# Softmax weights of the first batch four pipeline slots sooner, and q of pairs 2 to 5 (and 7) transposed by the DMA crossbar instead of TensorE

## The chip, the cores and the metric

One core of a Trainium2 chip runs the whole kernel. The metric is the device time of one execution in microseconds. Most executions of one kernel agree within 0.3%. A ratio is the mean time of one kernel's fast runs over that of the other's of the same rounds, so it is not quite the ratio of the medians quoted beside it. "By crossbar" means that a DMA transfer does the transpose (`dma_start_transpose`), so that neither TensorE nor VectorE works for it.

## The reference, cut to what matters

```python
# attention: batch 8, heads 8, seq 576, head_dim 64
scores = scale * q @ k.T
thresh = max(scores) - tau
attn   = softmax(where(scores >= thresh, scores, -1e9))
o      = attn @ v                                # [8, 8, 576, 64]
# layers on x = o as [4608, 512]
h   = x @ w_in                                   # [512, 2048]
out = (h - tanh(h)) @ w_out                      # [2048, 512]
```

## The kernel before

The unit of work is a **pair**, two heads of one batch; there are 32, four per batch. A pair has nine score tiles, and one tile goes through each stage of a software pipeline per **slot**. In slot s the kernel makes scores of tile s+8, applies the threshold to tile s+5 (`kink`, ScalarE), makes the softmax weights of tile s (`weights`: transposes on TensorE or by crossbar, then an exponential on ScalarE) and attends with tile s-2. From slot 40 on, the layers of the finished batch are woven in.

Each pair needs preparation some slots ahead of its first tile: q and k are loaded, split into a high and a low half on GpSimd, and turned (transposed). Meanwhile the layer weights arrive in 16 pieces, which GpSimd casts to bf16.

```python
def split(p, t):                  # GpSimd, 2.6 us for each of q and k
    nc.gpsimd.tensor_scalar(...)                  # scale
    nc.gpsimd.tensor_copy(out=hl[:, :, 0, :], ...)      # high half
    nc.gpsimd.tensor_tensor(out=hl[:, :, 1, :], ...)    # low half

def q_by_dma(p):
    return p >= 2 * HPAIR and p % 2 == 1          # HPAIR = 4

def turn(p, t):
    if t == "q" and q_by_dma(p):
        nc.sync.dma_start_transpose(...)          # SP queue
        return
    ...                                           # nine TensorE transposes
    nc.vector.tensor_copy(out=m, in_=ps)          # one VectorE copy
    ...

# one piece of layer weights every fourth slot: cast the last one, load the next
wt_pool = pool("wt", 2)
if s + AHEAD in w_when:
    if loaded:
        w_cast()                                  # GpSimd
    piece = next(pieces, None)
    if piece:
        w_load(piece)                             # SP queue
```

After the first pair, every load of q, k, v and layer weights, every crossbar transpose and every store (but for two of the last ones) is issued by one queue, SP. Where q goes by crossbar its `turn` stands five slots ahead of the pair's first scores, otherwise three.

Of the kernel before, what the change touches and what calls it, by code (L numbers as in the profile page):

```python
# [18 lines left out]
def kernel(  # L19
# [26 lines left out]
    HPAIR = H // 2  # L46
    NPAIR = B * HPAIR
    DM_C = d_model // P
    DF_C = d_ff // P
    TPP = 9  # L50
    NTILE = NPAIR * TPP
# [3 lines left out]
    def on_pe(i):  # L55
        p, j = divmod(i, TPP)
        return p < HPAIR or p < 2 * HPAIR and j in (0, 1, 4, 5, 6)
# [3 lines left out]
    AHEAD = 8  # L61
    LDK = 16
    MASK = 5
    LAG = 2
# [165 lines left out]

    def q_by_dma(p):

        return p >= 2 * HPAIR and p % 2 == 1

    def turn(p, t):
        hl = hls.pop((p, t))
# [48 lines left out]
    def kind(j):  # L285

        return "M" if j == 4 else "A" if j in (0, 2, 5, 7) else "B"
# [41 lines left out]
    def shift(i):  # L329

        kd = kind(i % TPP)
        if kd == "A":
            return
        n = 2 if kd == "B" else 1
        mx = mxs.pop(i)
        nb = st_pool.tile([P, 2], F32, name="nb", tag="nb")
        nc.vector.tensor_scalar(  # L337
            out=nb[:, 0:n], in0=mx[:, 0:n], scalar1=-1.0, scalar2=tau,
            op0=ALU.mult, op1=ALU.add,
        )  # L340
        nbs[i] = nb[:, n - 1 : n]
        if kd == "B":
            nbs[i - 1] = nb[:, 0:1]
# [23 lines left out]
    def weights(i):  # L367


        kd = kind(i % TPP)  # L370
        n, off = {"A": (4, 0), "M": (5, 0), "B": (5, 4)}[kd]
        if on_pe(i):
            z = zts.pop(i)
            pl, tag = (ps_h, "h") if i % 2 and i < HPAIR * TPP else (ps_y, "y")
            ps = pl.tile([P, 5 * P], BF16, name="psZ", tag=tag)
            for c in range(n):
                nc.tensor.matmul(  # L377
                    out=ps[:, c * P : (c + 1) * P],
                    lhsT=z[:, (off + c) * P : (off + c + 1) * P],
                    rhs=ident_bf, is_transpose=True, start=True, stop=True,  # L380
                )
            if kd == "B":
                pt = pts.pop(i - 1)
            else:
                pt = p_pool.tile([P, TPP * P], FP16, name="pT")
            nc.scalar.activation(  # L386
                out=pt[:, off * P : (off + n) * P], in_=ps[:, 0 : n * P], func=ACT.Exp
            )
        elif kd == "A":
            return  # L390
        else:
            n += off
            pt = p_pool.tile([P, TPP * P], FP16, name="pT")
            nc.scalar.activation(  # L394
                out=pt[:, 0 : n * P], in_=zts.pop(i)[:, 0:n, :], func=ACT.Exp
            )
        pts[i] = pt

    def attend(i):

        p, j = divmod(i, TPP)
        kd, vb = kind(j), vbs[p % NV]
        if kd == "A":
            return
        if j in (1, 6):
            ops[p, int(j > 4)] = ps_o.tile([P, 6, D + 1], F32, name="psO", tag="o")
        po = ops[p, int(j > 4)]
        if kd == "M":
            pt = pts.pop(i)

            for c in range(5):
                nc.tensor.matmul(  # L412
                    out=po[:, 4:6, :], lhsT=pt[:, c * P : (c + 1) * P],
                    rhs=vb[:, :, c, :], start=(c == 0), stop=(c == 4),
                )
            return
        pt, hh = pts.pop(i), int(j > 4)

        for ab in range(2):
            blocks = [(4 * ab + ab + c, c) for c in range(4)]  # L420
            blocks.append((4, 4 + ab))
            for n, (blk, c) in enumerate(blocks):
                nc.tensor.matmul(  # L423
                    out=po[:, (j - 1 - 5 * hh) + ab, :],
                    lhsT=pt[:, blk * P : (blk + 1) * P], rhs=vb[:, hh, c, :],
                    start=(n == 0), stop=(n == 4),
                )
# [3 lines left out]
    def norm(p, hh):  # L431
        po = ops.pop((p, hh))
        if hh == 0:
            osb[p] = o_pool.tile([P, 5, 2, D], BF16, name="osb")
        n = 5 - hh
        rc = st_pool.tile([P, 5], F32, name="rc", tag="rc")
        nc.vector.reciprocal(out=rc[:, 0:n], in_=po[:, 0:n, D])
        nc.vector.tensor_tensor(  # L438
            out=osb[p][:, 0:4, hh, :], in0=po[:, 0:4, 0:D],
            in1=rc[:, 0:4].unsqueeze(2).to_broadcast([P, 4, D]), op=ALU.mult,  # L440
        )
        if hh == 0:
            nc.vector.scalar_tensor_tensor(
                out=osb[p][:, 4, :, :], in0=po[:, 4:6, 0:D], scalar=rc[:, 4:5],
                in1=own, op0=ALU.mult, op1=ALU.mult,
            )
# [3 lines left out]
    def emit_x(p):  # L450
        o = osb.pop(p)
        pf = ps_h.tile([P, 320], F32, name="psX", tag="h")
        ps = pf[:, 0:256].bitcast(BF16)
        for t in range(4):
            nc.tensor.matmul(
                out=ps[:, t * P : (t + 1) * P],
                lhsT=o[:, t, :, :].rearrange("p a d -> p (a d)"),
                rhs=ident_bf, is_transpose=True, start=True, stop=True,
            )

        nc.tensor.matmul(
            out=pf[:, 256:320], lhsT=o[:, 4, :, :].rearrange("p a d -> p (a d)"),
            rhs=fold, start=True, stop=True,
        )
        b = p // HPAIR
        if p % HPAIR == 0:
            xs[b] = x_pool.tile([P, DM_C, MB], BF16, name="xT")
        nc.vector.tensor_copy(out=xs[b][:, p % HPAIR, :], in_=ps[:, 0:512])
        nc.vector.tensor_copy(out=xR[:, p % HPAIR, b, :], in_=pf[:, 256:320])
# [17 lines left out]
    def bend():  # L487
        while halves:
            m, n, ps = halves.pop(0)
            th = t_pool.tile([P, MB], F32, name="th")  # L490
            nc.scalar.activation(out=th, in_=ps, func=ACT.Tanh)  # L491
            ths.append((m, n, ps, th))

    def shrink():
        while ths:
            m, n, ps, th = ths.pop(0)
            nc.vector.scalar_tensor_tensor(  # L497
                out=gs[m][:, n, :], in0=th, scalar=-1.0, in1=ps,
                op0=ALU.mult, op1=ALU.add,
            )  # L500
# [102 lines left out]
    def w_cast():  # L603
        flat, wt, i, cols = loaded.pop(0)
        nc.gpsimd.tensor_copy(out=flat[:, i * cols : (i + 1) * cols], in_=wt)
# [51 lines left out]
        if at < -AHEAD:  # L657
            plan.setdefault(-AHEAD, []).extend(plan.pop(at))

    kinks = {}  # L660
    for i in range(NTILE):
        kinks.setdefault(i // 2 * 2 + 2 - AHEAD if i < 4 else i - MASK, []).append(i)
    for s in range(-AHEAD, NTILE + LAG + 3):
        p, j = divmod(max(s, 0), TPP)
        if 0 <= s < NTILE and j == 2 + LAG and p % HPAIR == 0 and p >= HPAIR:
            assert not todo
            todo = layers(stage, False)
            share = len(todo) / (HPAIR * TPP - 2 - LAG)
            done, stage = 0.0, stage + 1
        if 0 <= s + AHEAD - 1 < NTILE:  # L670
            shift(s + AHEAD - 1)
        if 0 <= s + AHEAD < NTILE:
            scores(s + AHEAD)
        if s == 1 - AHEAD:
            for t in ("k", "q", "ks"):
                turn_first(t, 1)
        for i in kinks.pop(s, []):
            kink(i)
        bend()
        if 0 <= s < NTILE:  # L680
            weights(s)
            if todo:
                done += share
                if j == TPP - 1 and p % HPAIR == HPAIR - 1:
                    done = 1e9
                while todo and done >= 1:
                    todo.pop(0)()
                    done -= 1
        if s == 0:
            nc.vector.tensor_tensor(  # L690
                out=fold, in0=ident_bf[:, 0:64], in1=ident_bf[:, 64:P], op=ALU.add
            )
        shrink()
        for store in stores[:-1]:
            store()
        del stores[:-1]
        if 0 <= s - LAG < NTILE:
            attend(s - LAG)
            pp, jj = divmod(s - LAG, TPP)
            if jj == 4:  # L700
                norm(pp, 0)
            if jj == 8:
                norm(pp, 1)
        pp, jj = divmod(s - LAG, TPP)
        if jj == 1 and 0 < pp <= NPAIR:
            emit_x(pp - 1)
        for step in plan.pop(s, []):
            step()
        if True:
            if s + AHEAD in w_when:  # L710
                if loaded:
                    w_cast()
                piece = next(pieces, None)
                if piece:
                    w_load(piece)
# [47 lines left out]
```

## Time and profile before

| | before |
|---|---|
| median, lowest, highest of 3 runs | 545.71, 544.46, 546.08 us |
| span of the profiled run | 542.9 us |
| TensorE, VectorE, ScalarE, GpSimd busy | 93%, 82%, 81%, 54% |
| first batch (no layers yet) | about 7 to 72 us |
| GpSimd in 19 to 40 us | 19.88 of 21 us |

### The profile page before, as it was taken

To read this page: it belongs to the slowest core of one execution; us is meant where nothing else is said; L and a number is where in the kernel's file an instruction comes from. 1 tells how busy PE (TensorE), PEld (TensorE's weight loads), DVE (VectorE), ACT (ScalarE), POOL (GpSimd) and SP (SyncE) were. 2 spreads that over 40 slices of the span, in tenths; PEclk is the share of its full clock that TensorE was granted. 3 is DMA by queue.
4 is the path that set the end of the run, shared out by engine and by line. 5 is a ranking of instruction groups with operands and counts; after the bars stand their busy time and mean duration, and the time that the engine had idled before them with its cause. 6 is when DMAs were issued, how large, how long until landed. Compare 5 with 4: busy or idle time off the path is not lost.

```text
span 542.9 us, 12962 instructions
## 1 busy us (share of the span) xinstructions
PE 507.5 (93%) x4722; PEld 290.3 (53%) x4790; DVE 447.1 (82%) x1196; ACT 439.3 (81%) x630; POOL 290.7 (54%) x390
## 2 busy tenths in 40 slices
PE   5888888889999899999999999999999999899997
PEld 3566655555555555555555555555555555444444
DVE  4999999898888899889988989989989988544440
ACT  4899999998898888889888989899888989633330
POOL 7899987765456666557555755666655730000000
PEclk9999999998999999999999999999999999999999
DMA  7554688679697988789988999999999965310103
GB/s 211 168 182 145 205 202 175 148 131 197 141 173 160 175 169 199 163 191 195 181 188 172 177 200 186 165 171 191 192 177 179 200 127 117 83 41 39 40 39 77
DMA packets 202239, 85.13 MB, mean 157 GB/s; under 512 B 169792, under 2 KB 194624, under 8 KB 202176
## 3 DMA queue, kind: packets, MB, share of 16 engines
q1 hardware_dynamic: 201584, 83.89, 72.7%
q8 instruction: 37, 0.61, 0.5%
q10 hardware_dynamic: 592, 0.43, 0.3%
q14 instruction: 26, 0.21, 0.1%
HBM read 36.70 MB, written 9.44 MB: 85 GB/s over the span
## 4 chain that ended last, share of the span: by engine, by line
PE 67%; DVE 19%; POOL 6%; ACT 4%; issue 3%; DMA 0%; ACTq 0%; SPq 0%; DVEq 0%; POOLq 0%
PE psY L504 19%; PE psH L478 17%; PE psS L313 14%; DVE sc L323 9%; PE psO L423 5%; DVE g L497 3%; PE psS L303 3%; PE ps_k L227 3%; PE psHt L478 3%; DVE nb L337 2%; ACT z L357 2%; DVE osb L438 1%; POOL kS L256 1%; PE ps_q L227 1%; PE psO L412 1%
## 5 line engine op out<-in xcount | busy, mean ns | idle before, releaser
L323 DVE TENSOR_SCALAR_CACHE_REDUCE sc<-psS 128x576 f32<-128x576 f32 x288 | 215.3, 749 | 16.4 <-PE psS L313 11.0
L357 ACT ACTIVATE z<-sc,nb 128x576 bf16<-128x576 f32 x256 | 194.2, 771 | 21.9 <-DVE nb L337 21.3
L256 POOL COPY kS<-kT 64x1152 f16<-64x1152 f16 x62 | 70.9, 1143 | 135.8 <-DVE nb L337 133.2
L504 PE MATMUL psY<-w_out_sb,g 128*128 128x512 bf16 (+1 forms) x556 | 138.4, 373 | 2.2 <-issue 0.8
L394 ACT ACTIVATE pT<-zT 128x1152 f16<-128x1152 bf16 (+1 forms) x128 | 137.3, 1073 | 0.0
L478 PE MATMUL psH<-xT,w_in_sb 128*128 128x512 bf16 x451 | 118.0, 379 | 6.5 <-DVE g L497 4.4
L313 PE MATMUL psS<-kT,qT 128*128 128x512 f16 (+1 forms) x512 | 105.6, 288 | 11.2 <-DVE sc L323 9.2
L491 ACT ACTIVATE th<-psH 128x512 f32<-128x512 f32 x128 | 75.5, 590 | 39.2 <-PE psH L478 37.0
L313 PEld LDWEIGHTS <-qT 128*128 128x128 f16 x1024 | 73.1, 98 | 61.3 <-issue 14.5
L497 DVE SCALAR_TENSOR_TENSOR g<-th,psH 128x512 bf16<-128x512 f32 x128 | 87.2, 681 | 18.4 <-ACT th L491 18.4
L313 PE MATMUL psS<-kS,qT 128*128 128x512 f16 x496 | 101.9, 287 | 0.1
L478 PEld LDWEIGHTS <-w_in_sb 128*128 128x128 bf16 x576 | 49.4, 98 | 60.7 <-issue 7.2
L504 PEld LDWEIGHTS <-g 128*128 128x128 bf16 x592 | 51.0, 98 | 56.6 <-issue 2.9
L423 PEld LDWEIGHTS <-pT 128*128 128x128 f16 x1280 | 55.7, 98 | 25.0 <-issue 1.4
L423 PE MATMUL psO<-vb,pT 128*128 128x65 bf16 x1280 | 61.5, 194 | 0.9 <-ACT pT L394 0.6
L337 DVE TENSOR_SCALAR nb<-mx 128x2 f32<-128x2 f32 (+1 forms) x160 | 49.1, 307 | 2.5
L386 ACT ACTIVATE pT<-psZ 128x640 f16<-128x640 bf16 (+1 forms) x56 | 37.6, 671 | 5.1 <-PE psZ L377 5.0
L180 POOL TENSOR_TENSOR qhl<-qraw,qhl 128x576 f16<-128x576 f32 x31 | 39.7, 1281 | 2.6
L180 POOL TENSOR_TENSOR khl<-kraw,khl 128x576 f16<-128x576 f32 x31 | 39.7, 1281 | 2.6
L250 DVE COPY kT<-ps_k 128x1152 f16<-128x1152 f16 x31 | 23.4, 756 | 13.6 <-PE ps_k L227 13.2
L514 DVE COPY yo<-psY 128x512 f32<-128x512 f32 (+1 forms) x31 | 21.1, 679 | 11.3 <-PE psY L504 6.4
L438 DVE TENSOR_TENSOR osb<-psO,rc 128x256 bf16<-128x256 f32 x64 | 27.2, 424 | 2.2
(77 smaller groups left out, 508.4 us busy)
## 6 DMA issues: line engine op xcount, KB each, us to landing
vraw<-in_v_dram SPq DMA_DIRECT2D x32, 256.0 KB, 3.4
out_dram<-yo SPq DMA_DIRECT2D x32, 256.0 KB, 3.0
kraw<-in_k_dram SPq DMA_DIRECT2D x31, 256.0 KB, 3.2
qraw<-in_q_dram SPq DMA_DIRECT2D x31, 256.0 KB, 3.6
wt<-in_moe_w_in_dram SPq DMA_DIRECT2D x8, 512.0 KB, 4.7
wt<-in_moe_w_out_dram SPq DMA_DIRECT2D x8, 512.0 KB, 4.1
zT<-z SPq DMA_TRANSPOSE x104, 3.5
kraw<-in_k_dram SPq DMA_DIRECT2D x32, 32.0 KB, 2.8
```

The lines of the kernel that those rows point to most:

```text
L180: nc.gpsimd.tensor_tensor(out=hl[:, :, 1, :], in0=x, in1=hl[:, :, 0, :], op=ALU.subtract)
L256: nc.gpsimd.tensor_copy(out=o, in_=i)
L313: nc.tensor.matmul(out=ps[:, dst], lhsT=lhs, rhs=kk[:, src], start=(n == 0), stop=(n == 1),)
L323: nc.vector.tensor_scalar(out=sc, in0=ps[:, lo : lo + S], scalar1=SC, scalar2=None, op0=ALU.mult, op1=ALU.max, accum_out=mx[:, c : c + 1],)
L337: nc.vector.tensor_scalar(out=nb[:, 0:n], in0=mx[:, 0:n], scalar1=-1.0, scalar2=tau, op0=ALU.mult, op1=ALU.add,)
L357: nc.scalar.activation(out=z, in_=sc, func=ACT.Prelu, bias=nb, scale=1.0, alpha=STEEP)
L394: nc.scalar.activation(out=pt[:, 0 : n * P], in_=zts.pop(i)[:, 0:n, :], func=ACT.Exp)
L423: nc.tensor.matmul(out=po[:, (j - 1 - 5 * hh) + ab, :], lhsT=pt[:, blk * P : (blk + 1) * P], rhs=vb[:, hh, c, :], start=(n == 0), stop=(n ...
L478: nc.tensor.matmul(out=ps, lhsT=w_in_sb[:, c, n * P : (n + 1) * P], rhs=xs[m][:, c, :] if m < B else xR[:, c, :, :], start=(c == 0), stop= ...
L491: nc.scalar.activation(out=th, in_=ps, func=ACT.Tanh)
L497: nc.vector.scalar_tensor_tensor(out=gs[m][:, n, :], in0=th, scalar=-1.0, in1=ps, op0=ALU.mult, op1=ALU.add,)
L504: nc.tensor.matmul(out=ps, lhsT=gs[m][:, n, ms * P : (ms + 1) * P], rhs=w_out_sb[:, n, cols], start=(n == 0), stop=(n == DF_C - 1),)
```

## The change

Two things. Weights, attention and normalization of the first batch (36 tiles) move four slots sooner, to fill the pipeline's ramp, and so does the output of its pairs 0 to 2; that of pair 3 stays at slot 39. And q of pairs 2 to 5 goes by crossbar; by the wording of the condition pair 7 does too.

```diff
     def q_by_dma(p):
-        return p >= 2 * HPAIR and p % 2 == 1
+        return p in (2, 3, 4, 5) or p > 5 and p % 2 == 1
...
+    for i in range(NTILE + 3):
+        at = i - 4 if i < HPAIR * TPP else i
+        atts.setdefault(at + LAG, []).append(i)
+        if i < NTILE:
+            wts.setdefault(at, []).append(i)
...
+        for i in wts.pop(s, []):
+            weights(i)
         if 0 <= s < NTILE:
-            weights(s)
...
-        if 0 <= s - LAG < NTILE:
-            attend(s - LAG)
-        ...                     # norm and emit_x of tile s - LAG
+        for i in atts.pop(s, []):
+            ...                 # attend, norm and emit_x of tile i
```

More of the change, by code (lines that the diff above doesn't have):

```diff
@@ L658 @@
             plan.setdefault(-AHEAD, []).extend(plan.pop(at))
-    kinks = {}
-    for i in range(NTILE):
-        kinks.setdefault(i // 2 * 2 + 2 - AHEAD if i < 4 else i - MASK, []).append(i)
+    kinks, wts, atts = {}, {}, {}
+    for i in range(NTILE + 3):
[3 more added lines that the diff above has]
+            wts.setdefault(at, []).append(i)
+            kinks.setdefault(i // 2 * 2 + 2 - AHEAD if i < 4 else i - MASK, []).append(i)
     for s in range(-AHEAD, NTILE + LAG + 3):
@@ L696 @@
         del stores[:-1]
-        if 0 <= s - LAG < NTILE:
-            attend(s - LAG)
-            pp, jj = divmod(s - LAG, TPP)
-            if jj == 4:
-                norm(pp, 0)
-            if jj == 8:
-                norm(pp, 1)
-        pp, jj = divmod(s - LAG, TPP)
-        if jj == 1 and 0 < pp <= NPAIR:
-            emit_x(pp - 1)
+        for i in atts.pop(s, []):
+            pp, jj = divmod(i, TPP)
+            if i < NTILE:
+                attend(i)
+            if i < NTILE and jj in (4, 8):
+                norm(pp, int(jj > 4))
+            if jj == 1 and pp:
+                emit_x(pp - 1)
         for step in plan.pop(s, []):
```

## The prediction

> **What bounds the kernel now.** I read the busy shares by stretch first, then the chain of waits, then the time lines of GpSimd, of the DMA-issuing queue (SP) and of TensorE. A pair is two heads of one batch: nine score tiles, nine slots of the software pipeline. Pairs 0 to 3 are the first batch, before the layers start. Busy time by stretch (columns: PE, weight load, DVE, ACT, POOL, then clock, DMA share, GB/s), cut at the first scores of pairs 3, 4, 5 and 6:
>
> ```profile
> 41.70:53.40 11.70, 10.28 (x149) 7.64 (x149) 11.13 (x32) 10.69 (x19) 11.11 (x14) 1.00 0.55 167
> 53.40:65.20 11.80, 10.36 (x153) 7.72 (x151) 11.49 (x33) 11.57 (x20) 11.21 (x15) 1.00 0.67 191
> 65.20:79.30 14.10, 12.01 (x142) 8.04 (x144) 13.64 (x35) 12.95 (x21) 12.56 (x17) 1.00 0.85 190
> ```
>
> VectorE, ScalarE and GpSimd are all at 91 to 98% here: no engine can lose a microsecond unnoticed. In the stretch 128 to 187 us TensorE has 57.67 of 59 us, so from the third batch on TensorE sets the pace, and what the change wins or loses by about 94 us is carried to the end unaltered.
>
> The chain of waits between 37 and 73 us runs through GpSimd almost without a break. GpSimd's own time line (start, length):
>
> ```profile
> 37.33 1.28 POOL L180 TENSOR_TENSOR qhl<-qraw,qhl 128x576 f16<-128x576 f32 x1
> 38.67 2.33 POOL L256 COPY kS<-kT 64x1152 f16<-64x1152 f16 x2
> ...
> 42.33 2.03 POOL L605 CAST w_in_sb<-wt 128x1024 bf16<-128x1024 f32 x2
> ...
> 48.55 1.28 POOL L180 TENSOR_TENSOR qhl<-qraw,qhl 128x576 f16<-128x576 f32 x1
> ...
> 54.55 1.04 POOL L605 CAST w_in_sb<-wt 128x1024 bf16<-128x1024 f32 x1
> ...
> 59.78 1.28 POOL L180 TENSOR_TENSOR qhl<-qraw,qhl 128x576 f16<-128x576 f32 x1
> ```
>
> No line of it between 17.4 and 73.3 us carries an idle note. GpSimd makes q of pairs 3, 4 and 5 ready at 38.61, 49.83 and 61.06 us, and the change takes nothing from it. The two casts merged at 42.33 are those of slots 15 and 19; the one at 54.55 is slot 27's.
>
> The DMA-issuing queue, same stretch:
>
> ```profile
> 34.86 0.60 SPq L142 DMA_DIRECT2D vraw<-in_v_dram  x1
> 35.51 0.64 SPq L148 DMA_DIRECT2D vraw<-in_v_dram  x1
> 36.24 7.50 SPq L617 DMA_DIRECT2D wt<-in_moe_w_in_dram  x2
> ...
> 46.73 0.64 SPq L148 DMA_DIRECT2D vraw<-in_v_dram  x1
> 47.47 0.54 SPq L617 DMA_DIRECT2D wt<-in_moe_w_in_dram  x1
> ```
>
> The weight piece that slot 19 casts was issued at 36.24 (the second of that line waits for the first cast to end), the piece that slot 27 casts at 47.47, each just behind a load of v. Last, the issues (KB, then median us from issue to landing):
>
> ```profile
> wt<-in_moe_w_in_dram SPq DMA_DIRECT2D x8, 512.0 KB, 4.7
> ...
> qT<-qhl SPq DMA_TRANSPOSE x12, 3.4
> ```
>
> **What the Trainium skill says.** "VectorE: DVE Perf Modes", section "The three transpose paths", gives 390 ns for a 128x128 transpose on TensorE and 1309 ns by the crossbar: the crossbar is the slower path and is worth it only where the engines are the bound. The trace agrees in direction: nine blocks on TensorE take 0.66 us and a VectorE copy of 0.75 us; by crossbar 3.4 us to landing, 1.30 us of it on the issuing queue. "DMA: Bandwidth & Descriptors", section "Anatomy of one DMA", says that DMA engines do not wait on semaphores; the wait is on the issuing sequencer before dispatch. So a transfer whose input is late holds up every later issue of that queue. The trace shows such holds: the 7.50 us line above, and over the whole run 20.5 us in which weight loads wait on that queue for a GpSimd cast. "PSUM — Partial Sum Buffer", section "Engine vs sequencer instructions", calls GpSimd's queue strict FIFO: a cast that waits for its piece holds the splits of q and k behind it. The order of GpSimd's lines in the trace fits that.
>
> **The change part by part.**
>
> Part 1, crossbar. The new condition takes pairs 2, 3, 4, 5 and also 7 off TensorE; pairs 9, 11 and on were off already. Each saves nine transposes (0.66 us of TensorE) and a VectorE copy, 0.68 us in the back-to-back stream, so 5 x 0.68 = 3.4 us of VectorE, 2.7 of it in the first batch. It also ends TensorE's wait of 1.10 us for q of pair 3 at 38.67. The price is latency: q is usable only 3.4 us after GpSimd is done. With GpSimd unmoved that is 42.0, 53.3 and 64.5 us for pairs 3, 4, 5; the trace has their first score matmuls at 41.74, 53.40 and 65.18. So even undisturbed, part 1 wins at most 0.7 us by pair 5.
>
> Part 2, order on the DMA-issuing queue. The transpose is put in five slots before the pair's last useful moment, ahead of the load of v two pairs on and of the next weight load. For pair 3 that is slot 14, ahead of slot 15's weight load. The queue now sits until 38.66, issues the transpose (1.30, to 39.96) and v (two issues, 1.3, to 41.3) and only then, at 41.35, the piece that left at 36.24 before. In the stretch 17 to 73 us such pieces land after 4.3 us: 45.65. Its cast stood at 43.35, so GpSimd idles 2.3 us. Everything behind moves: q of pair 4 is ready at 52.15. The same happens in slot 23: transpose, v and weight load follow at 52.2, and the piece lands 52.15 + 0.05 + 1.3 + 1.3 + 0.05 + 4.3 = 59.15; its cast would stand at 54.55 + 2.3 = 56.85, so another 2.3 us. Pair 2 (slot 5) does not do this: q is ready at 26.39, the piece would land at about 33.4, its cast stands at 34.83. Pair 5 does not either: between its transpose and the cast that needs the next piece lie the splits of pair 6, over 5 us. Sum on GpSimd: +4.6 us by pair 5, whose q is ready at 61.06 + 4.6 = 65.7 and lands at 69.1, against scores at 65.18: **+3.9 us**.
>
> Part 3, softmax weights four slots sooner. ScalarE has idle gaps of 1.04, 1.45 and 0.82 us between 12.8 and 19 us; four exponentials of about 0.55 us fill 2.2 us of them. After that it runs at the same rate as before, so until slot 32 nothing is won. In slots 32 to 35 no weights are made: 2.3 us of ScalarE and about 1 us of TensorE fall away, and the normalization of pair 3's second head (0.55 us of VectorE) leaves the stretch after pair 5's start. The layers still start at slot 40 and pair 3's output is still emitted at slot 39. Since engines are then waiting for q anyway, only the 0.55 counts, with perhaps 0.3 of waits: -0.8 from 69.1 on.
>
> Sum: +3.9 at the first scores of pair 5; -0.8 over the next nine slots (part 3); -0.7 when pair 7's q leaves VectorE (GpSimd is busy 39.86 of 55 us between 73 and 128 us, no longer late). That makes +2.4 by 94 us. 545.7 + 2.4 = 548.1; I say **548.0**.
>
> **The rivals.**
> A: no chain on the issuing queue (weight pieces arrive in time). Then the crossbar's latency still pins pairs 3 to 5, and the gain is 0.7 + 0.8 + 0.7, about -2: 543.6. For it: GpSimd's casts might be slack in a way I misjudge. Against it: the queue's order is program order in the trace, and the margin is missed by 2.3 us, not by tenths.
> B: VectorE is the bound and counts in full: -2.7 in the first batch, -0.7 for pair 7, plus waits: -4, 541.7. For it: 11.5 of 11.8 us busy. Against it: GpSimd without an idle line from 17 to 73 us.
> C: weights directly behind their kinks couple ScalarE and TensorE within one slot instead of five; every stall of one stops the other. ScalarE already waits for these transposes 3.0 us in 6 places. Some 0.1 us in each of 30 slots would be +3. But TensorE then only waits less for q, so it mostly hides under part 2: 548 to 551.
> D: crossbar landing at 5.0 us (the longest of the twelve) and pieces at 6.1 (the longest of sixteen): the loss doubles to about +5.5, 551.
>
> **Range and chances.** The main line gives 548, A 543.6, C and D up to 551; runs of before spread 1.6 us. Range 544.5 to 551.0. Two per cent is 10.9 us, which no rival reaches: faster 0.01, same 0.98, slower 0.01.
>
> **What would show it.** In the changed profile: (1) two idle notes of about 2.3 us on GpSimd's weight casts, released by the DMA of the piece, near 43 and 57 us; (2) waits of the issuing queue's q transposes for GpSimd's split; (3) TensorE's score matmuls waiting for the crossbar's q at the starts of pairs 3, 4, 5, near 42, 55.6 and 69 us; (4) 14 q copies on VectorE instead of 19, 17 q transposes by DMA instead of 12; (5) the same pace from pair 8 on, shifted by 2 to 3 us; (6) no ScalarE idle from 16 to 19 us. I am wrong if GpSimd shows no such idle, if the first scores of pair 5 start before 66 us, or if the shift is not there by 94 us but comes later.

## The result, and the profile after

| | before | after |
|---|---|---|
| median (4 runs each) | 545.53 us | 548.47 us |
| ratio, 95% interval | | 1.0058 (1.0040 to 1.0075) |
| span of the profiled run | 542.9 us | 546.6 us |
| first scores of pairs 3, 4, 5, 6, 7 | 41.74, 53.40, 65.18, 79.27, 93.31 us | 41.77, 55.08, 69.76, 83.79, 96.85 us |
| output of pair 31 taken up by VectorE | 472.49 us | 475.89 us |

(The fourth run of the kernel before was made with those of the changed kernel; hence 545.53 here and 545.71 above.)

The change made the kernel 0.6% slower, clear of noise. The last rows say when: nothing is lost at pair 3, 1.7 us at pair 4, 4.6 at pair 5; one microsecond comes back at pair 7; the rest stays to the end.

The same three stretches as in the prediction, busy time of PE, weight load, DVE, ACT, POOL, then clock, DMA share and GB/s, kernel after:

```profile
41.70:53.40 11.70, 9.53 (x110) 6.70 (x111) 7.31 (x23) 8.34 (x15) 9.14 (x12) 0.85 0.57 169
53.40:65.20 11.80, 8.37 (x109) 5.76 (x108) 8.07 (x26) 9.74 (x16) 7.77 (x12) 0.90 0.78 227
65.20:79.30 14.10, 12.43 (x125) 7.80 (x125) 10.95 (x33) 10.27 (x16) 13.45 (x16) 0.85 0.76 164
```

In the middle stretch VectorE fell from 11.49 to 8.07 us and GpSimd from 11.21 to 7.77: nobody is the bound, everybody waits. The seventh value, the clock, is below 1 in all three. The time line of GpSimd, kernel after, with the idle time before an instruction and its releaser in brackets:

```profile
42.15 1.04 POOL L605 CAST w_in_sb<-wt 128x1024 bf16<-128x1024 f32 x1
45.22 1.04 POOL L605 CAST w_in_sb<-wt 128x1024 bf16<-128x1024 f32 x1 [2.03 <-DMA wt<-in_moe_w_in_dram]
...
59.97 1.04 POOL L605 CAST w_in_sb<-wt 128x1024 bf16<-128x1024 f32 x1 [3.61 <-DMA wt<-in_moe_w_in_dram]
```

These two casts wait for a weight piece, 5.64 us together; before, neither waited. Why the pieces are late stands in the issuing queue's time line, kernel after:

```profile
38.45 1.33 SPq L239 DMA_TRANSPOSE qT<-qhl  x1
39.83 0.58 SPq L142 DMA_DIRECT2D vraw<-in_v_dram  x1
40.46 0.65 SPq L148 DMA_DIRECT2D vraw<-in_v_dram  x1
41.16 2.40 SPq L617 DMA_DIRECT2D wt<-in_moe_w_in_dram  x2
...
51.75 1.33 SPq L239 DMA_TRANSPOSE qT<-qhl  x1
53.12 0.58 SPq L142 DMA_DIRECT2D vraw<-in_v_dram  x1
53.75 0.65 SPq L148 DMA_DIRECT2D vraw<-in_v_dram  x1
54.45 0.59 SPq L617 DMA_DIRECT2D wt<-in_moe_w_in_dram  x1
```

The queue's loads of q end at 34.66; then it stands still until GpSimd's split of q is done at 38.43, issues the transpose, v, and only at 41.16 the piece that left at 36.24 before. It is the same 13 us later. TensorE, kernel after, shows who pays:

```profile
49.05 1.14 PE L227 MATMUL ps_k<-ident_f,khl 128*128 128x128 f16 x9 [2.01 <-POOL khl L180]
49.98 0.68 PE L313 MATMUL psS<-kT,qT 128*128 128x512 f16 x2
...
63.79 1.14 PE L227 MATMUL ps_k<-ident_f,khl 128*128 128x128 f16 x9 [2.94 <-POOL khl L180]
...
75.61 0.38 PE L377 MATMUL psZ<-ident_bf,z 128*128 128x128 bf16 x4 [1.34 <-ACT pT L386]
```

TensorE waits 2.01 and 2.94 us for the split of **k**, which stands behind the starved cast in GpSimd's queue; the crossbar's q comes later and just in time: issued at 51.75 and 66.49, it lands 3.3 and 3.2 us later, within 0.1 us of the first scores of pairs 4 and 5. The second line is a small lesson in reading: two score matmuls take 0.68 us there and 0.41 elsewhere, because TensorE's clock fell (0.57 of full speed in 49 to 53 us, and again in 62 to 70). Not every such pause brings this: one of 3.05 us in run 7 (at 30.64) was followed by full speed. The last line is a wait that the prediction lacks: a crossbar transpose of tile 39's weights stands in the issuing queue behind q and v (it is issued at 69.25 and lands at 73.11), ScalarE takes it up at 73.14, and TensorE waits for ScalarE. How much that transfer delays is not shown: ScalarE was busy until 73.02.

### The profile page after: what moved, and what is told of

The parts are those of the page before. It is cut to its first block, busy times and chain, and to the rows that moved or that the text cites. A ratio compares the mean times of both kernels' runs of the same rounds, so it can differ in the third digit from the quotient of the medians.

```text
span 546.6 us, 12874 instructions
## 1 busy us (share of the span) xinstructions
PE 507.8 (93%) x4677; PEld 288.8 (53%) x4745; DVE 441.6 (81%) x1191; ACT 439.3 (80%) x630; POOL 290.6 (53%) x390
## 4 chain that ended last, share of the span: by engine, by line
PE 67%; DVE 18%; DMA 4%; POOL 4%; issue 4%; ACT 2%; SPq 0%; DVEq 0%; POOLq 0%; ACTq 0%
PE psY L504 19%; PE psH L478 17%; PE psS L313 15%; DVE sc L323 8%; PE psO L423 5%; DVE g L497 3%; PE ps_k L227 3%; PE psS L303 3%; PE psHt L478 3%; DVE nb L337 2%; DMA zT<-z 2%; PE ps_q L227 1%; DVE osb L438 1%; PE psO L412 1%; POOL kS L256 1%
## 5 line engine op out<-in xcount | busy, mean ns | idle before, releaser
L313 PE MATMUL psS<-kT,qT 128*128 128x512 f16 (+1 forms) x512 | 106.7, 290 | 8.6 <-DVE sc L323 5.6
L337 DVE TENSOR_SCALAR nb<-mx 128x2 f32<-128x2 f32 (+1 forms) x160 | 46.1, 288 | 2.5
L227 PE MATMUL ps_k<-ident_f,khl 128*128 128x128 f16 x288 | 22.9, 227 | 10.4 <-DVE khl L193 5.4
```

The source lines that it names most:

```text
L313: nc.tensor.matmul(out=ps[:, dst], lhsT=lhs, rhs=kk[:, src], start=(n == 0), stop=(n == 1),)
L337: nc.vector.tensor_scalar(out=nb[:, 0:n], in0=mx[:, 0:n], scalar1=-1.0, scalar2=tau, op0=ALU.mult, op1=ALU.add,)
```

## The experiments

Three theories. **Theory 1**: q's transpose holds the issuing queue until GpSimd has split q; the weight piece behind it comes late, its cast stops GpSimd, and everything that GpSimd makes comes late. **Theory 2**: the crossbar's latency is the cost by itself. **Theory 3**: weights directly behind their kinks couple ScalarE and TensorE too tightly.

**Run 1: pieces loaded one further ahead.** The changed kernel, with the casts where they were:

```diff
-    wt_pool = pool("wt", 2)
+    wt_pool = pool("wt", 3)
...
-                if loaded:
+                if loaded and s + AHEAD > w_when[0]:
                     w_cast()
-                piece = next(pieces, None)
-                if piece:
-                    w_load(piece)
+                for _ in range(2 if s + AHEAD == w_when[0] else 1):
+                    piece = next(pieces, None)
+                    if piece:
+                        w_load(piece)
```

> The changed kernel with a third buffer for weight pieces, and the pieces loaded one further ahead (two at the first place, then one each), casts where they were. Theory 1, the issuing queue starves the casts: the two idle stretches of GpSimd before its casts (2.03 and 3.61 us) are gone, first scores of pair 5 at 64.5 to 65.5 us in place of 69.8, time 543.5 to 545.0, ratio to before 0.996 to 0.999. Theory 2, the latency of q by crossbar costs the time by itself: 547.5 to 548.5, ratio 1.004 to 1.006. Theory 3, weights too close behind their kinks: also 547.5 to 548.5.

Measured: 542.52 us, ratio 0.9957 (0.9945 to 0.9969). GpSimd's time line, run 1, over the first of the two places:

```profile
42.08 2.02 POOL L605 CAST w_in_sb<-wt 128x1024 bf16<-128x1024 f32 x2
44.08 0.67 POOL L176 TENSOR_SCALAR kraw<-kraw 128x576 f32<-128x576 f32 x1
```

The two casts run back to back and the split of k follows. The queue still stands still for q (its transposes are issued at 38.40, 49.60 and 60.80), but no cast starves. First scores of pair 5 are at 64.04. So the loss, and a little more than was expected, goes with the starved casts; theory 2 as the cause of the loss and theory 3 fall here. One buffer more turns the change from a loss into a gain.

**Run 2: crossbar alone.** Only the line of `q_by_dma`; weights at their old slots.

> Only q of pairs 2 to 5 and 7 by crossbar; softmax weights and attention at their old slots. Theories 1 and 2: the loss is all here, 548.5 to 549.5, ratio 1.005 to 1.008, both GpSimd idle stretches present at 2 us or more. Theory 3: back at 545 to 546, ratio 0.999 to 1.001.

Measured: 550.47 us, ratio 1.0106 (1.0088 to 1.0124), worse than expected. The casts wait 1.26 us (2 or more were expected) and 4.60 us, together 5.86. The loss is all in this part, and larger than in the full change.

**Run 3: weights alone.** The changed kernel with the old `q_by_dma`.

> Only the softmax weights and attention of the first batch four slots sooner; q as in the kernel before. Theories 1 and 2: a small gain, 544.3 to 545.5, ratio 0.998 to 1.000, GpSimd without an idle line between 20 and 70 us. Theory 3: 547 to 549, ratio 1.003 to 1.007.

Measured: 543.57 us, ratio 0.9974 (0.9962 to 0.9986): a gain of 0.26%, 1.4 us, more than expected, and against theory 3 again. GpSimd has no idle line between 20 and 70 us.

**Run 4: the hold alone, first try.** The kernel before, q by TensorE as before, plus a tiny transfer that needs q's split, where the crossbar's transpose would stand:

```diff
+    def hold(p):
+        nc.sync.dma_start(out=held, in_=hls[p, "q"][:, 0, 0, 0:32])
...
+        if p in (2, 3, 4, 5):
+            plan.setdefault(first - 5, []).append(lambda p=p: hold(p))
```

> The kernel before, q of all pairs up to 8 by TensorE as it was, plus one tiny transfer (64 bytes a partition) on the issuing queue that reads q's split of pairs 2 to 5, put where the changed kernel puts the crossbar transposes: it holds the queue until GpSimd has made q, and nothing else. Theory 1: most of the loss comes without any crossbar, 547 to 549, ratio 1.003 to 1.007, two GpSimd idle stretches before casts of 1 to 3 us (the transfer's issue is 0.7 us shorter). Theory 2: no loss, 545 to 546, ratio 0.999 to 1.001.

Measured: 544.97 us, ratio 1.0001 (0.9988 to 1.0013). By the letter this favours theory 2, but the experiment missed its aim. The transfer reads the high half of the split only, which GpSimd writes 1.28 us before the low half, and it issues in 0.51 us instead of 1.33. The queue was free 1.5 us sooner (the piece left at 39.62 instead of 41.16), and the casts waited 0.34 and 1.09 us, 1.43 in place of 5.64. So much of a delay the kernel bears.

**Run 5: the hold at full length.** As run 4, but reading the half that is made last, twice:

```diff
+    def hold(p):
+        for a in range(2):
+            nc.sync.dma_start(out=held[:, a], in_=hls[p, "q"][:, :, 1, :])
```

> The hold of before again, made as long as the crossbar's: the queue copies the low half of q's split (made last) of pairs 2 to 5 twice, so it waits for the whole split and issues for about 1.2 us; q itself still goes by TensorE as in the kernel before. Run four's hold waited only for the first half of the split, freed the queue 1.6 us sooner, and its casts waited 0.34 and 1.09 us only. Theory 1: GpSimd idles 2 and 3 us or more before the same two casts and the time is 547 to 550, ratio 1.004 to 1.009. Theory 2 (crossbar latency): idle stretches may be there but the time stays 544.5 to 545.5, ratio 0.999 to 1.002.

Measured: 552.67 us, ratio 1.0129 (1.0112 to 1.0145), slower than either theory said and the slowest of all, without one crossbar transpose more than the kernel before. GpSimd's time line, run 5:

```profile
46.23 1.04 POOL L611 CAST w_in_sb<-wt 128x1024 bf16<-128x1024 f32 x1 [2.72 <-DMA wt<-in_moe_w_in_dram]
...
61.55 1.04 POOL L611 CAST w_in_sb<-wt 128x1024 bf16<-128x1024 f32 x1 [4.18 <-DMA wt<-in_moe_w_in_dram]
```

The same two casts, 6.90 us. Waiting on the issuing queue makes the loss without any crossbar (that the extra copies are not to blame, run 12 shows). That it is larger than with crossbar alone fits the longer idle (6.90 against 5.86 us) and q's copies, which stay on VectorE here; the two were not taken apart.

**Run 6: control, pieces ahead in the kernel before.** The edit of run 1 on the kernel before.

> Control: the kernel before with the weight pieces one further ahead and nothing else. Its casts never waited for a piece, so theories 1 and 2 both say no change: 544.3 to 545.3, ratio 0.998 to 1.001. If loading ahead helps by itself, 543.5 or less, and then the verdict of the first run is too strong.

Measured: 545.61 us, ratio 1.0005 (0.9992 to 1.0018). Loading ahead gives nothing where nothing starves, so run 1's gain over the change is the starvation taken away and not a merit of the third buffer.

**Run 7: crossbar alone, pieces ahead.** Run 2 with the edit of run 1.

> Crossbar alone with the pieces one further ahead, softmax weights at their old slots. Theory 1: the loss of 1.06 per cent of crossbar alone is gone but for the latency, 543.8 to 545.5, ratio 0.998 to 1.001. Theory 2: 548 or more stays, ratio over 1.006.

Measured: 544.52 us, ratio 0.9983 (0.9970 to 0.9997). The loss of 1.06% has become a gain of 0.17%.

**Run 8: casts by the transfer.** The changed kernel with the layer weights cast in flight by transfers issued from GpSimd's queue; no cast on GpSimd, no piece on the SP queue:

```diff
-            nc.sync.dma_start(out=wt, in_=s)
-        loaded.append((flat, wt, i, cols))
+            nc.gpsimd.dma_start(out=dst, in_=s)       # dst: the bf16 weights
```

> The changed kernel with the layer weights cast by the transfer itself, issued from GpSimd's queue, no cast on GpSimd and no weight piece on the SP queue. Theory 1: GpSimd loses 16 casts of 1.04 us and the hold has nothing to starve, so 540 to 543, ratio 0.991 to 0.997, if the issue of such a transfer costs GpSimd less than the cast. If its issue costs as much as the cast (1 us or more), 543 to 545.

Measured: 545.41 us, ratio 1.0004 (0.9987 to 1.0021), no gain on the kernel before and a miss. An issue takes GpSimd 0.53 to 0.80 us (its time line), not nothing against the 1.04 of a cast. TensorE, run 8, at the start of pair 5:

```profile
65.86 0.66 PE L313 MATMUL psS<-kT,qT 128*128 128x512 f16 x2 [2.49 <-DMA qT<-qhl]
```

Here q by crossbar is late itself: issued at 60.02, landed 5.8 us later, where the longest in the changed kernel was 4.9; and TensorE's clock is 0.78 of full speed in 65.2 to 79.3 us. Whether the casting transfers slow the crossbar was not tried apart, so that stays open.

**Run 9: only the two pairs that starve a cast go back.** The changed kernel with `p in (2, 5)` in place of `p in (2, 3, 4, 5)`; two buffers, loads as before.

> The changed kernel with q of pairs 3 and 4 left to TensorE, so that only pairs 2, 5 and 7 are new on the crossbar; weight pieces loaded as before, two buffers. The prediction said that only the transposes of pairs 3 and 4 starve a cast. If so, no GpSimd idle of over 0.5 us before a cast between 20 and 70 us, and 542.5 to 544, ratio 0.995 to 0.998, near weights alone and the first run. If pair 2's and 5's holds starve casts too: 545 or more.

Measured: 542.25 us, ratio 0.9960 (0.9948 to 0.9971). The time is just under the expected 542.5 to 544, the ratio inside its range. One idle line of 0.24 us stands before a cast between 20 and 70 us. Pairs 2 and 5 hold the queue too, but the cast behind them is far enough away. A cast waits 2.26 us at 94 us, where GpSimd has time to spare, and it costs nothing that shows.

**Runs 10 and 11: versions meant to beat both.** Run 10 is run 1 with tiles 2 and 3 of pair 4 turned by TensorE, against the wait for tile 39's crossbar transpose:

```diff
-        return p < HPAIR or p < 2 * HPAIR and j in (0, 1, 4, 5, 6)
+        return p < HPAIR or i < HPAIR * TPP + 5 or p < 2 * HPAIR and j in (0, 1, 4, 5, 6)
```

> A version meant to beat both: the first run (pieces one further ahead) and, besides, tiles 2 and 3 of pair 4 transposed by TensorE instead of the crossbar, because in the first run ScalarE waited 0.84 us for that crossbar transfer at 67 us and TensorE 2.10 us behind it, where the four slots without weights end. If that wait is on the path: 541 to 542, ratio 0.992 to 0.9945. If it only delays what TensorE would wait for anyway: 542.3 to 543, ratio 0.995 to 0.997.

Measured: 542.53 us, ratio 0.9967 (0.9953 to 0.9981). The 2.10 us wait at 70 us is gone from the trace (the longest of that kind between 64 and 80 us is now 0.30), the time is not. That wait was taken over by others; the change isn't worth making. Run 11 adds q of pair 6 to the crossbar:

> The run before this one with q of pair 6 by crossbar too, so one more copy of 0.68 us leaves VectorE in the stretch where it is the busiest engine. If such a copy is worth its length there: 0.5 to 0.9 us less than the run before this one. If the latency of the crossbar or the issuing queue eats it: the same or up to 1 us more.

Measured: 543.48 us, ratio 0.9984 (0.9972 to 0.9997), if anything slower than run 10, as its second expectation had it. TensorE, run 11, at the start of pair 6:

```profile
80.45 0.42 PE L313 MATMUL psS<-kT,qT 128*128 128x512 f16 x2 [1.82 <-DMA qT<-qhl]
```

In run 10 the first scores of that pair wait for no crossbar. A copy saved on VectorE, 0.68 us, is paid with 1.82 us of latency.

**Run 12: full-length hold, pieces ahead.** Run 5 with the edit of run 1.

> The full-length hold of run five (queue waits for q's whole split and copies it twice, q itself by TensorE), now with the weight pieces one further ahead. If the hold does harm only by bringing weight pieces late to their casts: no GpSimd idle before a cast, 544.3 to 546, ratio 0.998 to 1.002. If the two extra copies of 147 KB or the hold of the k, q and v loads cost the time by themselves: over 549, ratio over 1.008, as in run five.

Measured: 545.83 us, ratio 1.0006 (0.9988 to 1.0024). The same holds and the same two extra copies as in the slowest run, and no loss that shows. Here a hold of the issuing queue costs nothing of its own; it costs what stands behind it and is needed soon.

Nine of the kernels form a table of ratios (weights sooner with pieces ahead, but no new crossbar, was not run):

| | pieces as before | pieces one further ahead |
|---|---|---|
| kernel before | 1.0000 | 1.0005 |
| weights four slots sooner | 0.9974 | |
| crossbar | 1.0106 | 0.9983 |
| both (the change) | 1.0058 | 0.9957 |
| hold of full length, no new crossbar | 1.0129 | 1.0006 |

Read across, the starvation costs 1.23% with crossbar alone (6.7 us of 545), 1.01% in the change (5.5 us) and 1.23% with the hold. Read down the right column, crossbar alone is worth 0.22%, 1.2 us. The shift of weights is worth 0.26% (1.4 us) both alone and beside crossbar with pieces ahead, and 0.48% (2.6 us) where casts starve. Weights alone were measured against the kernel before itself (0.9962 to 0.9986); the others are differences of two ratios whose intervals reach 0.12 to 0.18% to either side, so 0.22% and 0.26% there are not far from the noise. Runs 1 and 9 beat both kernels, at 542.5 and 542.3 us, and can't be told apart.

## Why the prediction was right

The predicted time was 548.0 us and the measured one 548.47; the cause that it named was the cause. Its steps:

- **The order on the issuing queue** (part 2). Right in mechanism and place: the two casts that it named, and not those behind pairs 2 and 5 (run 9). The size was low: 2.3 + 2.3 us were predicted, 2.03 + 3.61 came. The second piece was given 4.3 us to land, the median of such pieces, and took 5.4 (issued at 54.45, its cast starts at 59.97). The same piece, issued at 47.47, had taken 5.3 us in the kernel before: its own figure was the one to use, and the transfers issued right behind it now, between 55.24 and 57.72, need not have slowed it. Besides, GpSimd was free for its cast at 56.36, not at the 56.85 reckoned. The queue itself was met within half a microsecond: predicted issue of the first piece 41.35, measured 41.16.
- **First scores of pair 5 late by 3.9 us.** Measured 4.6, by the same step.
- **What TensorE would wait for.** The prediction expected its score matmuls to wait for the crossbar's q at pairs 3, 4 and 5. For pair 3 that pause stands there (the weight load of these scores waits 1.32 us for the crossbar); at pairs 4 and 5 TensorE stopped earlier, at the transposes of k, whose split is behind the same cast, and by the time of the scores q had just landed.
- **The crossbar's own worth** (part 1). Counted as at most 0.7 us by pair 5 and 0.7 at pair 7. Runs 6 and 7 give 1.2 us for all of it, and in the profile one microsecond comes back at pair 7.
- **The shift of weights** (part 3). Mis-sized: 0.8 us predicted, 1.4 to 2.6 measured. The idle gaps of ScalarE did fill: between 13.7 and 21.9 us only one idle of 0.18 us is left. Run 3 shows the step near where the prediction placed it: the scores of the middle tile of pair 4 begin at 58.09 us (57.70 before), those of pair 5 at 67.68 (70.30 before), and 1.5 us of this is left at pair 6 (83.95 and 85.50). In the profile of the change there is no such fall between pairs 5 and 6 (the lag is 4.6 and then 4.5 us). The wait for ScalarE behind tile 39's crossbar transpose lies there, but that it is the reason is not shown: run 10 took such a wait out of run 1 and won nothing.
- **The sum.** Two terms were wrong in opposite directions, the starvation too small by about a microsecond and the shift of weights too small by 0.6 to 1.8, so the close total is partly luck.
- **The rivals.** A, no chain on the queue, at 543.6: run 1 is that kernel, at 542.5. B, VectorE counting in full, at 541.7, was not reached by any version. C, the tight coupling, is refuted by run 3. D, slower landings, is what happened to the second piece, but not to q, which landed after 3.2 to 3.4 us at pairs 2 to 5. The carrying-over held: the lag is 3.5 us at pair 7 and 3.4 at pair 31.
- **Two loose readings**, which change nothing: GpSimd is at 89% in the third stretch, not above 91; and the 20.5 us of weight loads waiting for a cast are those of `w_in` alone, `w_out` adds 7.5.

One thing is left open: in the changed kernel the clock was lowered after the two pauses (the three stretches give 0.15 x 11.7 + 0.10 x 11.8 + 0.15 x 14.1, some 5 us of TensorE's time, against one such stretch in the kernel before). The runs with starved casts all have such pauses, so what the clock adds to the 5.64 us of GpSimd was not measured apart. Run 5 had one such stretch only and the largest loss, and pair 5's scores in the changed kernel begin when q lands, whose split waited for the cast and not for TensorE; both speak for a small share.

## What to carry to other kernels

When a transfer is moved to an in-order issuing queue, ask when its input is ready and what stands behind it: the harm of a queue that waits is done by the next transfers, to an engine that had nothing to do with the change. A buffer more, so that loads are issued a step before the hold, is the cheap cure; and before paying for the relief of one engine, look at which neighbour has no idle line in the stretch concerned.

## What the Trainium skill lacked or had wrong

- "DMA: Bandwidth & Descriptors", section "Rules for kernel authors", has no rule on ordering one queue's issues by when their inputs are ready; the section "Anatomy of one DMA" states only that the wait is on the issuing sequencer. Here such waits cost 1.23% (runs 2 and 7, runs 5 and 12), as far as the runs can tell all of it through a later, unrelated transfer that starved a GpSimd cast by up to 4.60 us.
- "VectorE: DVE Perf Modes", section "The three transpose paths", has one duration for a 128x128 crossbar transpose, 1309 ns. That section lacks the batched case and the split of the duration: nine blocks in one issue hold the issuing queue for 1.30 to 2.64 us and land after 3.2 to 4.9 us (kernel after), 5.8 us in run 8.
- "TensorE: Matmul & The Clock Gate", section "Part 1: The HAM clock gate (the "warmup" mystery)", puts the return to half clock after at least one idle window of about 3.4 us. In the kernel after, pauses of 2.01 and 2.94 us were enough: score matmuls right behind the first took 0.68 us a couple instead of 0.41. Pauses of 2.10 us (run 1, at 70 us), 2.28 us (run 5, at 50 us) and 3.05 us (run 7, at 31 us) were followed by full speed. So the length of the pause alone does not decide it.
